# Regrouping the small matmuls of a batch in a fused attention and gated feed-forward kernel

## The chip, the cores and the metric

The kernel runs on one core of one Trainium2 chip. The metric is device microseconds of one execution. The kernel before takes 305.18 us, the median of three runs (304.89, 305.18 and 305.53 us). The profile was taken of a further execution: its trace spans 302.9 us from the first to the last instruction.

In the profile, PE is TensorE's matmul, PEld its weight load, DVE is VectorE, ACT ScalarE, POOL GpSimd, and a name with a q at its end is that engine's sequencer issuing transfers. Every fp32 matmul of the program appears as two MATMUL records, so "x4" in a timeline row is two matmuls of the program.

## The reference

Two stages. The first is a linear attention over 4 batches of 4 heads, 1088 positions and 32 dimensions; its feature map is the product of two sketches of 8 rows. The second is a feed-forward block with a sigmoid gate over all 4352 tokens.

```python
def phi(x):                                   # S1, S2: 8 x 32
    a = np.einsum('rd,bhsd->bhsr', S1, x)
    b = np.einsum('rd,bhsd->bhsr', S2, x)
    return np.einsum('bhsi,bhsj->bhsij', a, b).reshape(*x.shape[:-1], r * r)
q_p, k_p = (phi(q), phi(k))
kv = np.einsum('bhsf,bhsd->bhfd', k_p, v)
z = np.sum(k_p, axis=2)
num = np.einsum('bhsf,bhfd->bhsd', q_p, kv)
den = np.einsum('bhsf,bhf->bhs', q_p, z)[..., None] + 1e-06
attn_out = num / den
# (B,H,S,D) -> x: 4352 tokens x 128
gate = 1.0 / (1.0 + np.exp(-(x @ w_gate)))    # 128 x 1536
val = x @ w_val
out = gate * val @ w_out                      # 1536 x 128
```

All data are fp32 for the computation. The weights come as 8-byte numbers and are narrowed to fp32 on the chip, in steps that VectorE, ScalarE and GpSimd share.

## The kernel before

The feed-forward block is cut into chunks of 512 tokens. A chunk has twelve **waves**: `w1` makes one block of 128 gate columns and 128 value columns (two matmuls of 128x512, into the two banks of a PSUM tile `wave`), ScalarE takes the sigmoid, VectorE multiplies (`g`), and `w2` adds the block's share of the output (one matmul of 128x512 into `moeout`), two waves later. A **slot** runs an optional group of attention work and then so many waves; the attention of the next batch is thus woven into the waves of the batch before it.

```python
    psm = ...tile_pool(name="psm", bufs=2, space=PSUM)   # tag "wave", [P, 2, 512]: two tiles
    pso = ...tile_pool(name="pso", bufs=1, space=PSUM)   # tags "acc0", "acc1": one bank each
    ps2 = ...tile_pool(name="ps2", bufs=1, space=PSUM)   # tag "two", [P, 2, 512]: one tile

    def slot(group, waves):
        if group is not None:
            group()
        todo = moe["todo"]
        for _ in range(waves):
            more = moe["ci"] < len(tok_chk)
            if more and sum(tok_chk[moe["ci"]]) > moe["ready"]:
                break
            glu()                       # VectorE: g = value * sigmoid(gate) of the last wave
            last = moe["ci"] == len(tok_chk) - 1 and moe["w"] > 1
            lag = 3 if last else 2
            while len(todo) >= lag:
                w2(*todo.pop(0))
            if more:
                w1()
            # ... (the end of the queue)
```

`w2` also turns a finished chunk out of PSUM with a VectorE transpose (`o_sb`) and writes it out.

For each batch after the first, the denominators of all positions are made in two small matmul groups with a VectorE product between them, and the numerators in two halves of 512 and 576 positions (`n` is 0 or 1). The last step divides and writes `xT`, the feed-forward input.

```python
    def den_j(b):
        glu()
        t = ps2.tile([P, 2, 512], F32, tag="two", name="denj")
        # ... 4 matmuls of 64x160 from ZW[b] and B8[b]
        PD[b] = sbA.tile([P, 2, WD], F32, tag="pd", name="pd", bufs=1)
        nc.vector.tensor_tensor(out=PD[b], in0=t[:, :, :WD], in1=A8[b], op=MUL)

    def den_i(b):
        dps = pso.tile([P, TCH], F32, tag=f"acc{(moe['sum'] + 1) % 2}", name="deni")
        # ... 4 matmuls of 32x160 from PD[b]
        return dps

    def turn_den(b, dps):               # transpose dTi, two additions of 1e-6, one reciprocal
        # ...

    def dn(b, n, mid=None):
        t0, tn = q_chk[n]
        # ... batch 0: matmuls of the denominators, dps
        elif n == 0:
            dps = den_i(b)
        # ...
        t = ps2.tile([P, 2, 512], F32, tag="two", name="nps")
        # ... 8 matmuls of 32x256 (n = 0) or 32x288 (n = 1) from ND[b] and QP[b]

        def divide(*parts, between=None):
            # ... n == 0: turn_den; batch 0: turn, add 1e-6, reciprocal of rc
            # transpose rb <- reciprocals (spread over 32 columns)
            # between()
            # xT <- t * rb
        return divide

    def part(b, n, between=None):
        glu()
        dn(b, n)(between=between)
```

The queries' feature map is made from `cq`, which goes to DRAM and comes back with each row repeated 8 times (`spread`, tiles `qp` and `bq`); `qmult(b, n)` multiplies the two in one half. The order of a batch:

```python
    slot(None, 1)
    slot(lambda: part(0, 1, lambda: narrow_w(NJ - 1, 3)), 2)   # last weight block's final step
    v_t[1] = load_v(1)
    for b in range(1, B):
        more = b + 1 < B
        wn = 1 if b == 1 else 2
        turn_k(b)
        turn_q(b, 0)
        slot(None, wn)
        turn_q(b, 1)
        slot(lambda: begin(b), 1)
        # ... feature map of the keys, sums over positions, kv
        qmult(b, 0)
        weights_z(b)
        slot(lambda: ndt(b), 1)
        qmult(b, 1)
        load_kq(b + 1)
        slot(lambda: den_j(b), 1)
        slot(lambda: part(b, 0), wn)
        slot(None, 1)
        slot(lambda: part(b, 1), 4)
    slot(None, 10**3)
```

`narrow_w(NJ - 1, 3)` is the last of four steps that narrow the twelfth weight block; the twelfth wave reads that block.

Of the kernel before, what the change touches and what calls it, by code (L numbers as in the profile page):

```python
# [8 lines left out]
F32 = mybir.dt.float32  # L9
# [5 lines left out]
MUL = ALU.mult  # L15

P = 128
# [3 lines left out]
def kernel(  # L21
# [12 lines left out]
    nc = tc.nc  # L34

    B, H, S, D = q.shape
    R = S1.shape[0]
# [3 lines left out]
    NJ = DFF // P  # L41
# [19 lines left out]
    psm = ctx.enter_context(tc.tile_pool(name="psm", bufs=2, space=bass.MemoryType.PSUM))  # L61
# [113 lines left out]
    def narrow_w(j, step):  # L175
        if not 0 <= j < NJ:
            return
        n, jj = divmod(j, 2)
        if wide:
            if step == 0:  # L180
                narrowing[j] = narrow(
                    w_sb[:, :, j, :], w_in[n][:, :, jj], nc.gpsimd, "acc1" if j < NJ - 2 else None
                )
            next(narrowing[j])
# [205 lines left out]
    def glu():  # L390
        if moe["gate"] is not None:
            moe["gate"]()
            moe["gate"] = None
# [223 lines left out]
    def spread(b, ns, cq, put, get):  # L617
        p0 = 64 * ns[0]
        d = dram.tile([P, 2, W1], F32, tag="dq", name="dq")
        put.dma_start(out=d[p0:], in_=cq[p0:])  # L620
        for n in ns:
            for c in range(2):
                for i, t in enumerate((QP[b], BQ[b])):
                    d0 = d[64 * n + 32 * c + 2 * i, 0]
                    rows = [[8 * W1, R], [0, R]] if i == 0 else [[0, R], [8 * W1, R]]
                    get.dma_start(  # L626
                        out=t[64 * c : 64 * c + 64, n * H * W1 : (n + 1) * H * W1],
                        in_=bass.AP(
                            tensor=d0.tensor, offset=d0.offset, ap=rows + [[1, H * W1]]
                        ),  # L630
                    )

        if len(ns) < 2:
            return


        B8[b] = sbA.tile([P, W1], F32, tag="b8", name="b8", bufs=1)
        A8[b] = sbA.tile([P, 2, WD], F32, tag="a8", name="a8", bufs=1)
        for x in range(2):
            for m in range(2):  # L640
                p0 = 64 * x + 32 * m
                for i, t in enumerate((A8[b], B8[b])):
                    d0 = d[2 * i + m, 0]
                    if i == 0:
                        offset, run = d0.offset + (W1 - WD) * x, [[W1, 2], [1, WD]]
                    else:
                        offset, run = d0.offset + W1 * x, [[1, W1]]
                    put.dma_start(
                        out=t[p0 : p0 + 32],
                        in_=bass.AP(tensor=d0.tensor, offset=offset, ap=[[8 * W1, 32]] + run),  # L650
                    )
# [138 lines left out]


    def den_j(b):
        glu()
        t = ps2.tile([P, 2, 512], F32, tag="two", name="denj")
        for pi in range(2):
            rows = slice(64 * pi, 64 * pi + 64)
            for x in range(2):
                nc.tensor.matmul(  # L798
                    out=t[64 * x : 64 * x + 64, pi, :WD],
                    lhsT=ZW[b][rows].rearrange("p x i -> p (x i)"),  # L800
                    rhs=B8[b][rows, (W1 - WD) * x : (W1 - WD) * x + WD],
                    start=True,
                    stop=True,
# [7 lines that stand above are left out]
        for h in range(H):  # L811
            nc.tensor.matmul(
                out=dps[32 * h : 32 * h + 32, :WD],
                lhsT=mask["head"][:, h % 2, :],
                rhs=PD[b][:, h // 2, :],
                start=True,
                stop=True,
            )
        return dps
# [12 lines left out]
        nc.vector.reciprocal(out=RC[b], in_=RC[b])  # L832


    def dn(b, n, mid=None):
        t0, tn = q_chk[n]
        w = 32 * tn
        if b == 0:
            bank = (moe["sum"] + 1) % 2 if moe["sum"] >= 0 else 1
            dps = pso.tile([P, TCH], F32, tag=f"acc{bank}", name="dps")  # L840
        elif n == 0:
            dps = den_i(b)
        for h in range(H if b == 0 else 0):
            nc.tensor.matmul(
                out=dps[32 * h : 32 * h + 32, :w],
                lhsT=zb[:, h, :],
                rhs=half(QP[b], n)[:, 2 * (h % 2) + h // 2, :],
                start=True,
                stop=True,
            )  # L850
        if b == 0:
            dT = sbA.tile([P, 9, 32], F32, tag="dT", name="dT")
            rc = sbA.tile([P, 9, 2], F32, tag="rc", name="rc")

        def turn():
            nc.vector.transpose(out=dT[:, :tn].rearrange("p t c -> p (t c)"), in_=dps[:, :w])

        if mid is not None:
            mid(turn, rc, dT)
        t = ps2.tile([P, 2, 512], F32, tag="two", name="nps")  # L860
        for h in range(H):
            for c in range(2):
                rows = slice(64 * c, 64 * c + 64)
                nc.tensor.matmul(  # L864
                    out=t[32 * h : 32 * h + 32, c, :w],
                    lhsT=ND[b][rows, 32 * h : 32 * h + 32],
                    rhs=half(QP[b], n)[rows, 2 * (h % 2) + h // 2, :],
                    start=True,
                    stop=True,
                )  # L870

        def divide(*parts, between=None):
            if b > 0:
                if n == 0:
                    turn_den(b, dps)
                rd = RC[b][:, n]
            else:
                rd = rc
                if mid is None:
                    turn()  # L880
                    nc.vector.tensor_scalar_add(rc[:, :tn], dT[:, :tn, :2], 1e-6)
                nc.vector.reciprocal(out=rc[:, :tn], in_=rc[:, :tn])
            rb = sbA.tile([P, 9, 2, 32], F32, tag="rb", name="rb")
            for u0, u1 in parts or [(0, tn)]:
                r0 = rd[:, u0:u1]
                nc.vector.transpose(
                    out=rb[:, u0:u1].rearrange("p t c s -> p (t c s)"),
                    in_=bass.AP(
                        tensor=r0.tensor,
                        offset=r0.offset,  # L890
                        ap=[list(r0.ap[0]), [1, 2 * (u1 - u0)], [0, 32]],
                    ),
                )
                if between is not None and u0 == 0:
                    between()
                o = b * S + 64 * (t0 + u0)
                nc.vector.tensor_tensor(  # L897
                    out=xT[:, o : o + 64 * (u1 - u0)].rearrange("p (t c s) -> p c t s", c=2, s=32),
                    in0=t[:, :, 32 * u0 : 32 * u1].rearrange("p c (t s) -> p c t s", s=32),
                    in1=rb[:, u0:u1].rearrange("p t c s -> p c t s"),  # L900
                    op=MUL,
                )
            moe["ready"] = b * S + 64 * (t0 + tn)

        return divide

# [108 lines left out]
    def q01():  # L1015
        spread(0, (1,), qcomp(0, (1,), (ps2, "two")), nc.scalar, nc.sync)

    def part(b, n, between=None):
        glu()
        dn(b, n)(between=between)  # L1020

    def kv_all(b):
        kv(b, ZS[b])
# [6 lines left out]
    qmult(0, 1)  # L1030
    load_kq(1)
    slot(None, 1)
    slot(lambda: part(0, 1, lambda: narrow_w(NJ - 1, 3)), 2)
    v_t[1] = load_v(1)
    for b in range(1, B):
        more = b + 1 < B
        wn = 1 if b == 1 else 2
        turn_k(b)
        turn_q(b, 0)
        slot(None, wn)  # L1040
        turn_q(b, 1)
        slot(lambda: begin(b), 1)
        for pi in range(2):
            outer(b, pi)
            slot(None, wn)
        for step in range(2):
            sum_z(b, step)
            slot(None, wn)
            if b == 1 and step == 0:
                masks()  # L1050
        slot(lambda: kv_all(b), wn)
        if more:
            v_t[b + 1] = load_v(b + 1)
        qmult(b, 0)
        weights_z(b)
        slot(lambda: ndt(b), 1)
        qmult(b, 1)
        load_kq(b + 1)
        slot(lambda: den_j(b), 1)
        slot(lambda: part(b, 0), wn)  # L1060
        slot(None, 1)
        slot(lambda: part(b, 1), 4)
    slot(None, 10**3)


# [28 lines left out]
```

## Time and profile before

| what | value |
|---|---|
| median of three runs | 305.18 us |
| span of the profiled execution | 302.9 us |
| VectorE busy | 154.6 us (51%) |
| ScalarE busy | 80.7 us (27%) |
| GpSimd busy | 36.4 us (12%) |
| TensorE clock granted, mean | 0.998 |
| 128x512 MATMUL records, wave and moeout | 436 and 216 |

A row of a timeline has the start in us, the duration in us, the engine, the line, the operation with its tiles and shape, the number of records merged in it, and, if the engine was idle before, for how long and what ended the wait. The duration of a matmul record is modelled and reaches past the start of the next one, because matmuls are pipelined; so lengths of work on TensorE are read here from start to start, not from durations.

The span has three parts. In the first 20 us the first inputs arrive, the first weights are narrowed and batch 0 is begun. From there to about 282 us waves follow one another, with the groups of the attention between them. The last chunk, of 256 tokens, ends it.

### The profile page before, as it was taken

The page shows a single profiled execution, that of the slowest core. Times are in us where ns is not written, and L with a number is a line of the kernel's source. Part 1 is how long each engine was busy: PE and PEld are TensorE (multiplying, and loading weights), DVE is VectorE, ACT ScalarE, POOL GpSimd, SP SyncE. Part 2 cuts the span into 40 slices and gives each one's busy share as a digit, 9 for nine tenths or more (in the row PEclk, how much of TensorE's full clock was granted, in tenths as well). Part 3 has the DMA queues.
Part 4 walks back from the last instruction along what each step waited for, and adds up shares of the span by engine and source line. Part 5 has one row for each costly group of instructions (what it writes and reads, how often), then busy time and mean ns, then how long its engine had stood idle before and what let it go on. Part 6 is the DMA issues. An engine that isn't in the chain of part 4 may idle for free.

```text
span 302.9 us, 3657 instructions
## 1 busy us (share of the span) xinstructions
PE 296.3 (98%) x1363; PEld 136.3 (45%) x1363; DVE 154.6 (51%) x268; ACT 80.7 (27%) x150; POOL 36.4 (12%) x68
## 2 busy tenths in 40 slices
PE   8899999999999999999999999999999999999995
PEld 3444433443444444434444444444444444444683
DVE  6997788774645554364465541744232223222331
ACT  2556532222122222221222222221222222222220
POOL 1465550610000410000002300000000000000000
PEclk9999999999999999999999999999999999999999
DMA  7993440898201494360013990200010000100011
GB/s 216 347 339 80 126 144 6 163 204 190 98 9 25 107 196 92 61 202 0 0 20 72 182 156 2 36 2 0 0 26 8 0 0 10 27 0 0 8 30 17
DMA packets 31411, 24.24 MB, mean 80 GB/s; under 512 B 21345, under 2 KB 26593, under 8 KB 31393
## 3 DMA queue, kind: packets, MB, share of 16 engines
q1 hardware_dynamic: 27024, 16.15, 20.6%
q0 software_dynamic: 3456, 7.09, 12.4%
q10 hardware_dynamic: 912, 0.77, 0.9%
q8 instruction: 11, 0.18, 0.3%
q14 instruction: 8, 0.06, 0.1%
HBM read 20.73 MB, written 3.26 MB: 79 GB/s over the span
## 4 chain that ended last, share of the span: by engine, by line
PE 84%; DMA 9%; DVE 3%; POOL 2%; issue 1%; SPq 1%; ACT 0%; POOLq 0%; ACTq 0%
PE wave L357 52%; PE moeout L314 27%; DMA v<-in_v_dram 3%; DMA w_in<-in_moe_w_out_dram 2%; DMA bq<-dq 2%; POOL head L118 2%; DMA w_in<-in_moe_w_gate_dram 1%; PE kvz L677 1%; PE nps L864 1%; DVE w_sb L127 1%; DVE head L109 1%; PE kps L456 1%; DVE head L105 0%; PE cqps L602 0%; PE denj L798 0%
## 5 line engine op out<-in xcount | busy, mean ns | idle before, releaser
L357 PE MATMUL wave<-xT,w_sb 128*128 128x512 f32 (+1 forms) x436 | 191.7, 565 | 0.1
L381 DVE TENSOR_TENSOR g<-wave,sg 128x512 f32<-128x512 f32 x102 | 70.3, 689 | 133.3 <-ACT sg L365 133.1
L357 PEld LDWEIGHTS wave<-xT,w_sb 128*128 128x128 f32 x436 | 82.6, 190 | 93.6 <-issue 86.3
L365 ACT ACTIVATE sg<-wave 128x512 f32<-128x512 f32 x102 | 60.9, 597 | 198.9 <-PE wave L357 198.9
L314 PE MATMUL moeout<-g,w_sb 128*128 128x512 f32 (+1 forms) x216 | 105.8, 577 | 0.3 <-DVE w_sb L127 0.3
L314 PEld LDWEIGHTS moeout<-g,w_sb 128*128 128x128 f32 x216 | 39.3, 190 | 44.0 <-issue 37.1
L626 POOL DMA_DIRECT2D qp<-dq x12 | 7.1, 591 | 108.4 <-DMA dq<-cq 68.4
L118 POOL TENSOR_TENSOR head<-head,tail 128x384 int32<-128x384 int32 (+2 forms) x14 | 13.4, 955 | 18.2 <-DVE head L109 14.0
L535 DVE TENSOR_TENSOR kp<-kab 128x1152 f32<-128x1152 f32 (+2 forms) x10 | 10.5, 1068 | 0.0
L655 DVE TENSOR_TENSOR qp<-qp,bq 128x1152 f32<-128x1152 f32 (+1 forms) x7 | 9.0, 1290 | 1.3 <-DMA bq<-dq 1.3
L109 DVE SCALAR_TENSOR_TENSOR head<-cap,head 128x384 int32<-128x384 int32 (+2 forms) x14 | 7.5, 535 | 0.5
L127 DVE SCALAR_TENSOR_TENSOR w_sb<-square,head 128x384 f32<-128x384 f32 (+1 forms) x11 | 5.7, 518 | 3.9 <-POOL head L118 3.9
L258 PE MATMUL warm<-const-float32-1.0 128*128 128x512 f32 (+1 forms) x12 | 6.9, 703 | 0.8 <-PEq L1078 0.8
L626 POOL DMA_DIRECT2D bq<-dq x12 | 6.9, 576 | 0.4 <-DVE g L381 0.2
L101 ACT ACTIVATE tail<-w_in 128x384 int32<-128x384 uint32 (+1 forms) x13 | 6.6, 522 | 0.9 <-DMA w_in<-in_moe_w_gate_dram 0.7
L324 DVE STREAM_TRANSPOSE o_sb<-moeout 128x512 f32<-128x512 f32 (+1 forms) x9 | 6.1, 679 | 1.4 <-PE moeout L314 1.3
L97 POOL TENSOR_SCALAR cap<-w_in 128x384 f32<-128x384 f32 (+1 forms) x13 | 6.5, 509 | 0.0
L897 DVE TENSOR_TENSOR xT<-nps,rb 128x576 f32<-128x576 f32 (+2 forms) x9 | 5.9, 660 | 0.7
L864 PE MATMUL nps<-qp,nd 64*32 64x256 f32 (+1 forms) x128 | 5.5, 401 | 0.4 <-ACT nd L741 0.4
L436 DVE STREAM_TRANSPOSE qT<-kq 128x512 f32<-128x512 f32 (+1 forms) x8 | 5.8, 719 | 0.0
L117 ACT ACTIVATE square<-cap 128x384 f32<-128x384 f32 (+1 forms) x11 | 5.1, 463 | 1.6 <-DVE w_sb L127 1.5
L425 DVE STREAM_TRANSPOSE kT<-kq 128x1088 f32<-128x1088 f32 (+2 forms) x5 | 5.3, 1070 | 0.0
(89 smaller groups left out, 85.3 us busy)
## 6 DMA issues: line engine op xcount, KB each, us to landing
qp<-dq POOLq DMA_DIRECT2D x12, 288.0 KB, 9.6
bq<-dq POOLq DMA_DIRECT2D x12, 288.0 KB, 10.3
v<-in_v_dram SPq DMA_DIRECT2D x16, 144.0 KB, 6.5
kq<-in_k_dram SPq DMA_DIRECT2D x3, 544.0 KB, 3.8
kq<-in_q_dram SPq DMA_DIRECT2D x3, 544.0 KB, 4.7
w_in<-in_moe_w_out_dram SPq DMA_DIRECT2D x6, 256.0 KB, 7.1
w_in<-in_moe_w_gate_dram SPq DMA_DIRECT2D x5, 256.0 KB, 5.8
w_in<-in_moe_w_val_dram SPq DMA_DIRECT2D x5, 256.0 KB, 4.7
```

Source lines behind the costliest of these rows:

```text
L109: nc.vector.scalar_tensor_tensor(out=head, in0=cap, scalar=-0x40000000, in1=head, op0=ALU.bitwise_and, op1=ALU.bitwise_or)
L118: nc.gpsimd.tensor_tensor(out=head, in0=head, in1=tail, op=ALU.add)
L127: nc.vector.scalar_tensor_tensor(out=out, in0=square, scalar=1.265625 * 2.0**-30, in1=head, op0=ALU.is_ge, op1=MUL)
L258: nc.tensor.matmul(out=t[:, 0, :n], lhsT=x, rhs=r, start=True, stop=True)
L314: nc.tensor.matmul(out=moe["acc"][:, :tw], lhsT=w_sb[:, 2, j, :], rhs=g[:, jj, :tw], start=(j == 0), stop=(j == NJ - 1),)
L357: nc.tensor.matmul(out=wv[:, which, jj * tw + o : jj * tw + o + tp], lhsT=w_sb[:, which, j0 + jj, :], rhs=xT[:, t0 + o : t0 + o + tp], sta ...
L365: nc.scalar.activation(out=sg, in_=wv[:, 0], func=ACTF.Sigmoid)
L381: nc.vector.tensor_tensor(out=g, in0=wv[:, 1], in1=sg, op=MUL)
L535: eng.tensor_tensor(out=KP[b][:, pi, j0:j1].rearrange("p j m (i l) -> p (j m) i l", i=R), in0=bass.AP(tensor=a0.tensor, offset=a0.offset, ...
L626: get.dma_start(out=t[64 * c : 64 * c + 64, n * H * W1 : (n + 1) * H * W1], in_=bass.AP(tensor=d0.tensor, offset=d0.offset, ap=rows + [[1, ...
L655: nc.vector.tensor_tensor(out=q0, in0=q0, in1=half(BQ[b], n), op=MUL)
L864: nc.tensor.matmul(out=t[32 * h : 32 * h + 32, c, :w], lhsT=ND[b][rows, 32 * h : 32 * h + 32], rhs=half(QP[b], n)[rows, 2 * (h % 2) + h // ...
```

## The change

The change does four things.

1. For each batch after the first, the small matmul groups are put together. Before, `denj` stood alone, then came a wave, then `deni` with the first numerators, then one or two waves and another, then the second numerators. Now one group holds `denj`, the second numerators, `deni` and the first numerators, in this order; the second numerators stand between `denj` and `deni`, and use a `wave` tile in PSUM so that both halves can be held at once.
2. In batch 1 this group comes one slot later than `denj` did. Also one VectorE transpose of the queries (`turn_q(1, 0)`) is put behind a slot.
3. In the spread of the queries, the rows of `qp` for both halves of the partitions come in one transfer of 128 partitions instead of two of 64. `bq` stays as it was.
4. At the end of batch 0, the final narrowing step of the twelfth weight block stands ahead of the reciprocal on VectorE, rather than behind the transpose that follows it. The division's last product is put behind the next `glu`.

The purpose is to have fewer changes between wide and small matmuls, and to have the twelfth weight block ready sooner. The diff, cut to its core:

```diff
@@ spread @@
-            for c in range(2):
-                for i, t in enumerate((QP[b], BQ[b])):
+            for i, t in enumerate((QP[b], BQ[b])):
+                for c in (0, 1) if i else (0,):
                     d0 = d[64 * n + 32 * c + 2 * i, 0]
-                    rows = [[8 * W1, R], [0, R]] if i == 0 else [[0, R], [8 * W1, R]]
+                    rows = [[0, R], [8 * W1, R]] if i else [[8 * W1, 2 * R], [0, R]]
                     get.dma_start(
-                        out=t[64 * c : 64 * c + 64, n * H * W1 : (n + 1) * H * W1],
+                        out=t[64 * c : 64 * c + 64 if i else P, n * H * W1 : (n + 1) * H * W1],
@@ den_j @@
-        glu()
         t = ps2.tile([P, 2, 512], F32, tag="two", name="denj")
@@ dn @@
-    def dn(b, n, mid=None):
+    def dn(b, n, mid=None, pool=(ps2, "two")):
-        elif n == 0:
-            dps = den_i(b)
-        t = ps2.tile([P, 2, 512], F32, tag="two", name="nps")
+        t = pool[0].tile([P, 2, 512], F32, tag=pool[1], name="nps")
@@ divide @@
-        def divide(*parts, between=None):
+        def divide(*parts, first=None, between=None, later=False):
-                if n == 0:
-                    turn_den(b, dps)
+                if first is not None:
+                    first()
                 nc.vector.reciprocal(out=rc[:, :tn], in_=rc[:, :tn])
 ...
+                if later and u1 == tn:
+                    return lambda: product(u0, u1)
+                product(u0, u1)
@@ order @@
-    def part(b, n, between=None):
+    def part01(first):
         glu()
-        dn(b, n)(between=between)
+        late.append(dn(0, 1)(first=first, later=True))
+    def last01():
+        glu()
+        late.pop()()
+    def parts(b):
+        den_j(b)
+        glu()
+        divide1 = dn(b, 1, pool=(psm, "wave"))
+        dps = den_i(b)
+        divide0 = dn(b, 0)
+        turn_den(b, dps)
+        divide1()
+        divide0()
 ...
-    slot(lambda: part(0, 1, lambda: narrow_w(NJ - 1, 3)), 2)
+    slot(lambda: part01(lambda: narrow_w(NJ - 1, 3)), 1)
+    slot(last01, 1)
 ...
-        turn_q(b, 0)
+        if b > 1:
+            turn_q(b, 0)
         slot(None, wn)
+        if b == 1:
+            turn_q(b, 0)
 ...
-        slot(lambda: den_j(b), 1)
-        slot(lambda: part(b, 0), wn)
-        slot(None, 1)
-        slot(lambda: part(b, 1), 4)
+        if b == 1:
+            slot(None, 1)
+        slot(lambda: parts(b), wn + 5)
```

More of the change, by code (lines that the diff above doesn't have):

```diff
@@ L881, in divide, with product @@
                     nc.vector.tensor_scalar_add(rc[:, :tn], dT[:, :tn, :2], 1e-6)
+                if first is not None:
+                    first()
                 nc.vector.reciprocal(out=rc[:, :tn], in_=rc[:, :tn])
             rb = sbA.tile([P, 9, 2, 32], F32, tag="rb", name="rb")
+            def product(u0, u1):
+                o = b * S + 64 * (t0 + u0)
+                nc.vector.tensor_tensor(
+                    out=xT[:, o : o + 64 * (u1 - u0)].rearrange("p (t c s) -> p c t s", c=2, s=32),
+                    in0=t[:, :, 32 * u0 : 32 * u1].rearrange("p c (t s) -> p c t s", s=32),
+                    in1=rb[:, u0:u1].rearrange("p t c s -> p c t s"),
+                    op=MUL,
+                )
+                moe["ready"] = max(moe["ready"], b * S + 64 * (t0 + u1))
             for u0, u1 in parts or [(0, tn)]:
@@ L895, in divide @@
                     between()
[L896 to L903, printed above, removed]
+                if later and u1 == tn:
+                    return lambda: product(u0, u1)
+                product(u0, u1)
         return divide
@@ L1016, in q01 @@
         spread(0, (1,), qcomp(0, (1,), (ps2, "two")), nc.scalar, nc.sync)
-    def part(b, n, between=None):
+    late = []
+    def part01(first):
         glu()
-        dn(b, n)(between=between)
+        late.append(dn(0, 1)(first=first, later=True))
[11 more added lines that the diff above has]
+        divide0()
     def kv_all(b):
```

## The prediction

> **What bounds the kernel now.** I read the page's busy table first, then the chain that ended last, then TensorE's timeline around one batch, and last all engines around the two places where the change moves VectorE work.
>
> ```profile
> PE 296.3 (98%) x1363; PEld 136.3 (45%) x1363; DVE 154.6 (51%) x268; ACT 80.7 (27%) x150; POOL 36.4 (12%) x68
> ...
> PE 84%; DMA 9%; DVE 3%; POOL 2%; issue 1%; SPq 1%; ACT 0%; POOLq 0%; ACTq 0%
> ```
>
> TensorE is busy for 98% of the span and makes up 84% of the chain; the rest of the chain is almost all in the first 45 us. So from there on a change counts only if it alters the time from one matmul to the next. Nothing that VectorE, GpSimd or a transfer saves is worth anything unless TensorE was waiting for it. TensorE's timeline in batch 1 (start, duration, line, records):
>
> ```profile
> 59.55 1.02 PE L314 MATMUL moeout<-g,w_sb 128*128 128x512 f32 x2
> ...
> 62.12 1.02 PE L314 MATMUL moeout<-g,w_sb 128*128 128x512 f32 x2
> ...
> 69.96 1.88 PE L357 MATMUL wave<-xT,w_sb 128*128 128x512 f32 x4
> 71.77 0.50 PE L798 MATMUL denj<-b,zw 64*64 64x160 f32 x8
> 72.20 1.13 PE L314 MATMUL moeout<-g,w_sb 128*128 128x512 f32 x2
> 73.17 1.88 PE L357 MATMUL wave<-xT,w_sb 128*128 128x512 f32 x4
> 74.98 0.48 PE L812 MATMUL deni<-pd,head 128*32 128x160 f32 x8
> 75.39 0.66 PE L864 MATMUL nps<-qp,nd 64*32 64x256 f32 x16
> 75.98 1.12 PE L314 MATMUL moeout<-g,w_sb 128*128 128x512 f32 x2
> 76.94 1.88 PE L357 MATMUL wave<-xT,w_sb 128*128 128x512 f32 x4
> ...
> 79.52 1.88 PE L357 MATMUL wave<-xT,w_sb 128*128 128x512 f32 x4
> 81.33 0.71 PE L864 MATMUL nps<-qp,nd 64*32 64x288 f32 x16
> 81.97 1.12 PE L314 MATMUL moeout<-g,w_sb 128*128 128x512 f32 x2
> 82.94 1.88 PE L357 MATMUL wave<-xT,w_sb 128*128 128x512 f32 x4
> ```
>
> An undisturbed wave takes 62.12 - 59.55 = 2.57 us start to start: 0.86 for moeout, 1.715 for wave. Where a small group follows, wave takes longer: 71.77 - 69.96 = 1.81, so going in costs 0.095. Where a wide matmul follows a small group, moeout takes 73.17 - 72.20 = 0.97 instead of 0.86, so coming out costs 0.11. No engine is waited for at these places; the price is of the change itself, about 0.205 us for each group however small.
>
> The second place is the end of batch 0 (all engines):
>
> ```profile
> 43.46 1.00 POOL L118 TENSOR_TENSOR head<-head,tail 128x384 int32<-128x384 int32 x1 [1.63 <-DVE head L109]
> ...
> 44.52 0.27 DVE L882 RECIPROCAL rc<-rc 128x18 f32<-128x18 f32 x1
> 44.82 0.78 DVE L886 STREAM_TRANSPOSE rb<-rc 128x576 f32<-128x576 f32 x1
> 44.97 1.02 PE L314 MATMUL moeout<-g,w_sb 128*128 128x512 f32 x2
> ...
> 45.52 0.52 DVE L127 SCALAR_TENSOR_TENSOR w_sb<-cap,head 128x384 f32<-128x384 f32 x1
> ...
> 46.10 1.98 PE L357 MATMUL wave<-xT,w_sb 128*128 128x512 f32 x4
> ```
>
> This wave is the twelfth, which reads the block that w_sb writes. It was due at 44.97 + 0.86 = 45.83, but starts at 46.10, 0.06 after w_sb ends at 46.04. The reader is to see that the modelled end of moeout (45.99) hides most of this wait. Its cost is 0.27 and 0.10 more in the wave that restarts (the next moeout is at 47.92, 1.82 after it instead of 1.715).
>
> **What the Trainium skill says.** "TensorEngine Tiling (Array Packing)", Key Properties: changing the tiling mode drains TensorE. The trace agrees in kind: denj is 64*64, nps 64*32, deni 128*32, the wide ones 128*128, and each way in and out costs the 0.095 and 0.11 above. "TensorE: Matmul & The Clock Gate", Step-by-step: TensorE loads weights ahead of running matmuls only where row groups don't conflict or the background buffer is free. The 190 ns loads lie beside matmuls here (45% busy under 98%), and can't all lie beside a group of 8 short ones. "Perfetto Trace Analysis", Tensor Engine Instruction: ends of matmuls are estimates; the 0.27 us above shows it, so I count starts. "DMA: Bandwidth & Descriptors", Issuing engines are not separate DMA queues: fewer issues save only the sequencer's time. Before, an issue of qp takes GpSimd 0.59 us on the page and nothing on TensorE waits behind it.
>
> **The change part by part.**
>
> *Grouping, before.* For batch 1, against waves with nothing between: denj costs 72.20 - 71.675 + 0.11 = 0.635 (the wave was due to end at 69.96 + 1.715). deni with nps costs 75.98 - 74.885 + 0.105 = 1.20. The second nps costs 81.97 - 81.235 + 0.11 = 0.845. Sum 2.68 us. Batches 2 and 3 show the same within 0.02.
>
> *Grouping, after.* The matmuls are the same in number and shape; what goes is two ways in and two out, 2 x 0.205 = 0.41. Against it stands a new wait: deni needs pd, VectorE's product of denj, which had a whole wave to be made in and now has only the second nps. Worked out from denj's start: its modelled end is at 0.50; ScalarE started 0.06 after such an end elsewhere (kvz ends 123.72, kvd starts 123.78); pd takes 0.48; another 0.06 back to TensorE, as for w_sb. So deni can start at 1.10. The second nps, from 0.43 to 0.43 + 0.64 = 1.07, fills all of it but 0.03. The group is then 0.095 + 1.10 + 0.41 (deni) + 0.59 (nps of 256) + 0.105 = 2.30, and a batch gains 2.68 - 2.30 = 0.38.
>
> *What VectorE must have ready.* The second nps reads what qmult(b, 1) writes. In batch 1 qmult waits for a transfer and ran from 71.81 to 73.17, after denj's start; in the new order denj comes one slot of 2.57 later, at about 74, so nothing waits. This is what the extra slot is for. In batch 2 qmult ran from 130.34 to 131.69, and denj starts at 131.68, nps 0.43 later: no wait. In batch 3:
>
> ```profile
> 190.25 0.71 DVE L324 STREAM_TRANSPOSE o_sb<-moeout 128x512 f32<-128x512 f32 x1
> ...
> 193.23 1.35 DVE L655 TENSOR_TENSOR qp<-qp,bq 128x1152 f32<-128x1152 f32 x1
> ```
>
> Here a chunk ended just before, and its transpose took VectorE's time. Batch 2 now spends 7 waves after denj, not 8, so in batch 3 the chunk's end falls a wave later, into the slot right ahead of the group. The queue is then: g after the sigmoid (ends at 192.19) to 192.85, o_sb to 193.5, qmult to 194.8. The second nps could start at 194.17 + 0.43 = 194.60, but starts at 194.86; pd, behind qmult, ends near 195.25, and deni starts near 195.5 rather than 195.27. That takes back 0.2, and leaves 0.18 in batch 3.
>
> *Buffers.* The second nps takes a wave tile. The wave two further on needs that tile, and so the second division's product. From deni's end VectorE has dTi 0.34, two additions 0.25, reciprocal 0.38, transpose 0.78 and product 0.76 with gaps of 0.04, near 2.8 us; TensorE comes back to the tile after nps, a wave and moeout, 0.6 + 2.68 + 0.86 = 4.1 us. No wait. deni's bank is wanted by moeout only where a chunk begins there, in batch 3; dTi is through about when nps ends, so at most 0.1.
>
> *Narrowing step.* w_sb at 44.52 instead of 45.52 ends at 45.04, long before 45.83: gain 0.37. The delayed product ends near 47.6; the wave that reads it is due at 48.4.
>
> *Transfers and the moved transpose.* 12 qp issues become 6. TensorE waits for none of them in the traces of batches 2 and 3. Counted as 0.
>
> Sum: 0.37 + 0.38 + 0.38 + 0.18 = 1.31 us. 305.18 - 1.31 = 303.87, say 303.9.
>
> **The rivals.** *The pd wait grows.* If the semaphore from TensorE to VectorE and back costs 0.3 more than I read, in each batch, all but 0.4 us of the gain is lost: 304.7. For it: pd never followed denj directly, so its start after denj isn't seen (in batch 2 it began at 133.03, behind g). Against it: the 0.06 at kvd. *The small groups get cheaper side by side.* If most of a switch's cost belongs to the wide weight load (190 ns), then denj and the second nps, now followed by narrow ones, shorten too, by up to 0.1 each; pd's wait would swallow most of it. That makes 303.6. *qmult becomes the bound in every batch.* If the transfers of bq land later than before, since qp's larger transfer stands ahead of them, batch 1's group waits: VectorE already idles 1.3 us for bq there. The new slot leaves about 1.2 us of room; beyond it TensorE would stall one for one, and 1 us lost gives 304.9. *Nothing is gained*, because TensorE's other waits take over: the list of what TensorE waited for has no row after 46 us (its largest, 0.8 us, is at the start), so I give this little.
>
> **Range and chances.** The terms that I trust are the 0.37 and the six ways in and out (1.23); the uncertain ones are waits of 0 to 0.3 a batch, and the medians' own spread of 0.3. I take 303.2 to 304.8. Two per cent is 6.1 us, four times all that the change touches on the chain; so faster 0.01, same 0.98, slower 0.01. That it is faster at all I hold at 0.88.
>
> **What would show it.** In the profile after: the twelfth wave 0.86 after its moeout (right) or a later start behind another VectorE row (wrong). In each batch one row sequence denj, nps, deni, nps with one start of moeout at 0.97 after it. deni 1.05 to 1.15 after denj in batches 1 and 2, and about 0.2 more in batch 3 with qmult just ahead. From the wave ahead of denj to the wave after nps, 2.30 above undisturbed waves in batches 1 and 2. It would be wrong if deni stood more than 0.3 later than said, if the second nps waited for qp in batch 1, or if a wave after the group waited for a division.

## The result, and the profile after

The changed kernel takes 303.49 us (median of four runs, 303.37 to 304.15), the kernel before beside it 305.03 (304.70 to 305.53). The ratio is 0.9952, with a 95% interval from 0.9932 to 0.9973: a gain of 0.8 to 2.1 us. A second comparison, on the chip of the last four experiments, gave 303.75 (nine runs) against 304.82 (33 runs), ratio 0.9965, from 0.9952 to 0.9979.

The page of the changed kernel, its busy table and its chain by engine:

```profile
PE 295.3 (98%) x1363; PEld 137.3 (46%) x1363; DVE 154.7 (51%) x268; ACT 80.7 (27%) x150; POOL 33.0 (11%) x62
...
PE 86%; DVE 5%; DMA 3%; issue 2%; POOL 2%; ACT 1%; SPq 0%; DVEq 0%; POOLq 0%; ACTq 0%
```

TensorE has as many records as before and is 1.0 us shorter busy. The modelled durations of neighbouring records overlap, so what went is not work but time from one start to the next. Its timeline around the group, in batch 1 and then only the group in batches 2 and 3:

```profile
72.11 1.88 PE L357 MATMUL wave<-xT,w_sb 128*128 128x512 f32 x4
73.92 0.50 PE L797 MATMUL denj<-b,zw 64*64 64x160 f32 x8
74.36 0.72 PE L861 MATMUL nps<-qp,nd 64*32 64x288 f32 x16
75.13 0.48 PE L811 MATMUL deni<-pd,head 128*32 128x160 f32 x8
75.54 0.66 PE L861 MATMUL nps<-qp,nd 64*32 64x256 f32 x16
76.13 1.13 PE L314 MATMUL moeout<-g,w_sb 128*128 128x512 f32 x2
77.09 1.88 PE L357 MATMUL wave<-xT,w_sb 128*128 128x512 f32 x4
...
130.99 0.50 PE L797 MATMUL denj<-b,zw 64*64 64x160 f32 x8
131.42 0.72 PE L861 MATMUL nps<-qp,nd 64*32 64x288 f32 x16
132.11 0.48 PE L811 MATMUL deni<-pd,head 128*32 128x160 f32 x8
132.52 0.66 PE L861 MATMUL nps<-qp,nd 64*32 64x256 f32 x16
...
190.54 0.50 PE L797 MATMUL denj<-b,zw 64*64 64x160 f32 x8
191.20 0.72 PE L861 MATMUL nps<-qp,nd 64*32 64x288 f32 x16 [0.15 <-DVE qp L655]
191.85 0.48 PE L811 MATMUL deni<-pd,head 128*32 128x160 f32 x8
192.26 0.66 PE L861 MATMUL nps<-qp,nd 64*32 64x256 f32 x16
```

There is one way in (72.11 to 73.92, 1.81) and one way out (76.13 to 77.09, 0.96). deni starts after denj by 1.21 us in batch 1, 1.12 in batch 2 and 1.31 in batch 3. All engines at the end of batch 0, and VectorE in batches 1 and 3:

```profile
44.44 0.56 DVE L127 SCALAR_TENSOR_TENSOR w_sb<-cap,head 128x384 f32<-128x384 f32 x1
44.91 0.26 DVE L881 RECIPROCAL rc<-rc 128x18 f32<-128x18 f32 x1
44.92 1.02 PE L314 MATMUL moeout<-g,w_sb 128*128 128x512 f32 x2
...
45.78 1.88 PE L357 MATMUL wave<-xT,w_sb 128*128 128x512 f32 x4
45.91 0.65 DVE L381 TENSOR_TENSOR g<-wave,sg 128x512 f32<-128x512 f32 x1
46.49 0.74 DVE L886 TENSOR_TENSOR xT<-nps,rb 128x576 f32<-128x576 f32 x1
...
70.01 1.35 DVE L655 TENSOR_TENSOR qp<-qp,bq 128x1152 f32<-128x1152 f32 x1
...
74.49 0.49 DVE L805 TENSOR_TENSOR pd<-denj,a 128x320 f32<-128x320 f32 x1 [1.72 <-DMA kq<-in_k_dram]
...
74.90 0.68 DVE L381 TENSOR_TENSOR g<-wave,sg 128x512 f32<-128x512 f32 x1
...
189.20 0.70 DVE L324 STREAM_TRANSPOSE o_sb<-moeout 128x512 f32<-128x512 f32 x1
189.83 1.32 DVE L655 TENSOR_TENSOR qp<-qp,bq 128x1152 f32<-128x1152 f32 x1
...
191.12 0.49 DVE L805 TENSOR_TENSOR pd<-denj,a 128x320 f32<-128x320 f32 x1
```

The twelfth wave starts 0.86 after its moeout. In batch 1 the product of the queries starts at 70.01 without a wait. In batch 3 it stands behind o_sb, ends at 191.15, and the second numerators start 0.05 after that.

One more step of the change belongs here, since deni waits for pd: `glu` now stands behind `den_j`, so on VectorE pd comes ahead of g (74.49 and 74.90). Before, g came first (in batch 2 at 132.42, pd at 133.03). No run tests this order by itself.

**How the runs are compared below.** A whole run contains a start-up whose length differs by chance: the first moeout started anywhere from 19.04 to 19.93 us in the fourteen profiles here, all of the same program up to there. So each run is judged by the time from the first moeout to the start of the last row of moeout, called its *length*. It covers everything that the change touches. The kernel before: 296.39 - 19.26 = 277.13. The changed kernel: 295.18 - 19.23 = 275.95; the same kernel a second time: 295.11 - 19.18 = 275.93. So the length repeats within 0.02 in these two, and the change is worth 1.18 us of it.

| run | length, us | against |
|---|---|---|
| before | 277.13 | |
| changed kernel | 275.95 | before: -1.18 |
| narrowing step alone | 276.83 | before: -0.30 |
| joined transfer alone | 277.09 | before: -0.04 |
| no slot in batch 1 | 275.94 | changed: -0.01 |
| no slot, two transfers | 275.96 | changed: +0.01 |
| slot, two transfers | 276.85 | changed: +0.90 |
| the same again | 275.94 | changed: -0.01 |
| group split | 277.06 | changed: +1.11 |
| deni straight behind denj | 277.22 | changed: +1.27 |
| queries' product early | 275.76 | changed: -0.19 |
| mask on VectorE | 275.86 | changed: -0.09 |
| both of these | 275.68 | changed: -0.27 |

### The profile page after: what moved, and what is told of

Same layout as the page of the kernel before. It is cut to its first block, busy times and chain, and to the rows that moved or that the text cites. A ratio compares the mean times of both kernels' runs of the same rounds, so it can differ in the third digit from the quotient of the medians.

```text
span 301.7 us, 3642 instructions
## 1 busy us (share of the span) xinstructions
PE 295.3 (98%) x1363; PEld 137.3 (46%) x1363; DVE 154.7 (51%) x268; ACT 80.7 (27%) x150; POOL 33.0 (11%) x62
## 3 DMA queue, kind: packets, MB, share of 16 engines
q0 software_dynamic: 2592, 7.08, 10.5%
## 4 chain that ended last, share of the span: by engine, by line
PE 86%; DVE 5%; DMA 3%; issue 2%; POOL 2%; ACT 1%; SPq 0%; DVEq 0%; POOLq 0%; ACTq 0%
PE wave L357 52%; PE moeout L314 27%; DMA bq<-dq 2%; PE nps L861 2%; POOL head L118 1%; PE kvz L677 1%; DVE head L109 1%; DVE w_sb L127 1%; DVE qp L655 1%; DMA s_in<-in_S_dram 1%; PE kps L456 1%; DVE head L105 1%; PE cqps L602 0%; PE deni L811 0%; PE dps L841 0%
## 5 line engine op out<-in xcount | busy, mean ns | idle before, releaser
L627 POOL DMA_DIRECT2D qp<-dq x6 | 3.5, 583 | 105.9 <-DMA dq<-cq 105.9
L535 DVE TENSOR_TENSOR kp<-kab 128x1152 f32<-128x1152 f32 (+2 forms) x10 | 10.5, 1070 | 0.0
```

The costliest lines, as they stand in the source:

```text
L535: eng.tensor_tensor(out=KP[b][:, pi, j0:j1].rearrange("p j m (i l) -> p (j m) i l", i=R), in0=bass.AP(tensor=a0.tensor, offset=a0.offset, ...
L627: get.dma_start(out=t[64 * c : 64 * c + 64 if i else P, n * H * W1 : (n + 1) * H * W1], in_=bass.AP(tensor=d0.tensor, offset=d0.offset, ap ...
```

## The experiments

### The narrowing step alone

On the kernel before; `first` is the narrowing step, and the division's last product stays ahead of g:

```diff
-        def divide(*parts, between=None):
+        def divide(*parts, between=None, first=None):
 ...
+                if first is not None:
+                    first()
                 nc.vector.reciprocal(out=rc[:, :tn], in_=rc[:, :tn])
 ...
-    def part(b, n, between=None):
+    def part(b, n, first=None):
         glu()
-        dn(b, n)(between=between)
+        dn(b, n)(first=first)
```

> The kernel before with one thing changed: the last narrowing step of the twelfth weight block ahead of the reciprocal. Theory: the twelfth wave starts 0.86 us after its moeout instead of 1.13, and the wave after it takes no extra 0.10; so from the start of the eleventh wave's moeout on everything on TensorE is 0.37 us earlier than in the kernel before, and the rest is as before. Rival: VectorE's delay is only moved, since the reciprocal and the transpose now run later and hold back the division that the first wave of the second chunk needs; then that wave starts late and the gain is below 0.1 us.

The length is 0.30 shorter. Of this, 0.03 lies ahead of the edited place: `dps`, a matmul group of batch 0, starts 21.73 us after the first moeout, in the kernel before 21.76. From the twelfth wave's moeout to kps of batch 1 it took 5.35 us instead of 5.62, a gain of 0.27: the twelfth wave was on time, but one 0.10 stayed. The timeline of this run:

```profile
45.53 0.19 PEld L357 LDWEIGHTS wave<-xT,w_sb 128*128 128x128 f32 x1 [0.24 <-DVE rc L884]
45.96 1.88 PE L357 MATMUL wave<-xT,w_sb 128*128 128x512 f32 x4
...
46.27 0.76 DVE L899 TENSOR_TENSOR xT<-nps,rb 128x576 f32<-128x576 f32 x1
46.95 0.68 DVE L381 TENSOR_TENSOR g<-wave,sg 128x512 f32<-128x512 f32 x1
...
47.68 0.30 PEld L314 LDWEIGHTS moeout<-g,w_sb 128*128 128x128 f32 x2 [0.67 <-DVE g L381]
47.68 1.12 PE L314 MATMUL moeout<-g,w_sb 128*128 128x512 f32 x2
48.64 1.88 PE L357 MATMUL wave<-xT,w_sb 128*128 128x512 f32 x4
```

moeout started when it was due (45.96 + 1.715), yet took 0.96 to the wave instead of 0.86. Its operand g, behind the division on VectorE, ended at 47.63, only 0.05 before. The weight load shows what is different: that of the wave at 45.96 starts 0.43 ahead of its matmul, that of this moeout waits for g and starts with it. In the changed kernel the division's last product is put behind g, g ends at 46.56, the load starts at 47.06 for a moeout at 47.49, and the 0.10 is gone: from moeout to kps it takes 5.24. The rival was right that VectorE's delay is moved, and wrong on what it hits and how hard; the deferred product, which the prediction valued at nothing, is worth this 0.10. It has no run of its own.

The same sign stands at every way out of a small group: the wide load starts with the moeout behind the group (in the changed kernel both at 76.13), where an undisturbed one starts 0.43 ahead, and in the kernel before at the wave that restarts late (load at 46.09, wave at 46.10). All of these lose about 0.10. A load that starts only 0.22 ahead loses nothing (36.27, wave at 36.49, next moeout 1.72 after it, in the kernel before). That the late load is what costs it fits all three places, but no run separates it from the change of shape.

### The transfers and the slot: four runs and a repeat

The joined transfer alone, on the kernel before:

```diff
-            for c in range(2):
-                for i, t in enumerate((QP[b], BQ[b])):
+            for i, t in enumerate((QP[b], BQ[b])):
+                for c in (0, 1) if i else (0,):
 ...
-                    rows = [[8 * W1, R], [0, R]] if i == 0 else [[0, R], [8 * W1, R]]
+                    rows = [[0, R], [8 * W1, R]] if i else [[8 * W1, 2 * R], [0, R]]
 ...
-                        out=t[64 * c : 64 * c + 64, n * H * W1 : (n + 1) * H * W1],
+                        out=t[64 * c : 64 * c + 64 if i else P, n * H * W1 : (n + 1) * H * W1],
```

> The kernel before with one thing changed: qp's rows in one transfer of 128 partitions. Theory: VectorE's wait for bq in batch 1 is gone, as in all runs with the joined transfer so far, but TensorE never waited for it in this order of groups; so from the first moeout to the last row of moeout TensorE takes the 277.13 us of the kernel before within 0.05. Rival: the joined transfer is worth something on TensorE by itself, 0.2 us or more.

Length 277.09, within 0.05 of before. The product in the kernel before, and then in this run:

```profile
71.81 1.36 DVE L655 TENSOR_TENSOR qp<-qp,bq 128x1152 f32<-128x1152 f32 x1 [1.30 <-DMA bq<-dq]
...
70.95 1.35 DVE L655 TENSOR_TENSOR qp<-qp,bq 128x1152 f32<-128x1152 f32 x1
```

VectorE's wait for bq was gone, and nothing was gained on TensorE.

The changed kernel without the slot:

```diff
-        if b == 1:
-            slot(None, 1)
-        slot(lambda: parts(b), wn + 5)
+        slot(lambda: parts(b), wn + 5 + (b == 1))
```

> The changed kernel without the extra slot in batch 1: the group of small matmuls stands a wave earlier, at about 71.35 us, and the waves after it are one more. Theory 1 (the joined transfer of qp brings bq earlier, the product of the queries in batch 1 ran from 70.01 to 71.36 us in the changed kernel and not from 71.8): the second numerators, due at 71.35 + 0.43 = 71.78 us, wait for nothing, and the end on TensorE is within 0.1 us of the changed kernel. Theory 2 (as the prediction had it: the slot is what spares the wait): the numerators wait about 1 us and the end is about 1 us later.

Length 275.94: denj at 71.53, the numerators at 71.97 as if nothing were to be waited for, since the product of the queries had ended at 71.54. Theory 1 holds, and with the joined transfer the slot does nothing in this run.

The same without the joined transfer (the diff above turned round as well):

> The changed kernel without the extra slot in batch 1 and with qp's rows in two transfers of 64 partitions as before. Theory 1 (the joined transfer brings bq earlier): the product of the queries in batch 1 waits for bq until about 71.4 us (71.8 in the kernel before, less the 0.43 gained by then) and ends at about 72.7; the second numerators, due at 71.8, start at about 72.8, so the end is 0.9 to 1.0 us later than with the joined transfer and no slot. Theory 2 (landing times of bq do not depend on how qp is cut): no difference from the run without the slot and with the joined transfer.

The product waited for bq, but only by 0.38, until 70.74; the numerators started 0.10 late and pd's wait behind them swallowed it (deni again 1.21 after denj). The length is the same, 0.02 apart, as theory 2 had it. The product did wait, as theory 1 had it, but too briefly to cost anything.

With the slot and without the joined transfer:

> The changed kernel with its extra slot in batch 1, but qp's rows in two transfers of 64 partitions as before. Theory 1: VectorE waits for bq in batch 1 by 1.0 to 1.5 us again, and TensorE does not, because the slot leaves 2.57 us; the end is within 0.1 us of the changed kernel. Theory 2 (the transfers are worth something on TensorE even with the slot): the end is 0.3 us or more later.

Here the wait was long:

```profile
69.74 0.69 DVE L381 TENSOR_TENSOR g<-wave,sg 128x512 f32<-128x512 f32 x1 [1.19 <-ACT sg L365]
...
73.70 1.36 DVE L654 TENSOR_TENSOR qp<-qp,bq 128x1152 f32<-128x1152 f32 x1 [3.27 <-DMA bq<-dq]
74.27 0.50 PE L796 MATMUL denj<-b,zw 64*64 64x160 f32 x8
...
74.98 0.68 DVE L381 TENSOR_TENSOR g<-wave,sg 128x512 f32<-128x512 f32 x1
...
75.72 0.72 PE L860 MATMUL nps<-qp,nd 64*32 64x288 f32 x16 [0.95 <-DVE g L381]
```

VectorE stood 3.27 us for bq, and g of a finished wave stood behind it in VectorE's order. The numerators want that wave's PSUM tile, so they start 0.06 after g's end (75.66), not after the product's (75.06). denj to nps is 1.45 us instead of 0.44. The end is 0.90 later, which is theory 2's outcome. Theory 1 had the wait at 1.0 to 1.5 us; it was longer than the slot could cover. Repeated and timed:

> The changed kernel with qp's rows in two transfers of 64 partitions, again and timed. In the single look it took 276.85 us from the first moeout to the last row of moeout, 0.90 more than the changed kernel, since VectorE waited 3.27 us for bq in batch 1; the run without the slot waited only 0.38. Theory 1 (with the two transfers the landing of bq in batch 1 differs from run to run by some us, by chance): the times of the rounds spread over 0.5 us or more, and their median is 0.2 to 1.0 us above the changed kernel's. Theory 2 (the long wait was a single event): the median is within 0.15 us of the changed kernel's.

The profile of the repeat has a wait of 1.97 us for bq and a length of 275.94, so the slot covered it: the product ended at 73.40 and the numerators started at 74.33. Without the slot they would have been due 2.57 earlier, so by these numbers an estimate of their wait there is 1.7 us. The median of 22 runs is 303.61, 0.14 below the changed kernel's, but four of the 22 lie at 304.56, 304.69, 304.94 and 307.36, while none of the changed kernel's 13 is above 304.16. So theory 2 is right on the median and theory 1 on the spread. The run with the wait of 3.27 took 304.78, like three of these four; but none of the four was profiled, so it isn't shown that bq made them late, and the slowest also had a lower mean clock (0.987).

In all, five profiles with two transfers show waits for bq of 1.30, 0.55, 0.38, 3.27 and 1.97 us, and nine profiles with the joined one show none. Counted from the first moeout, VectorE got bq at 51.2 to 54.1 us with two transfers, and with the joined one it was there at 50.8 us in eight of the nine profiles (in the ninth VectorE came for it only at 51.1). So the joined transfer lands bq earlier in these profiles and spares VectorE a wait of changing length, which made the length longer in one of the five. No profile with the joined transfer had bq late enough to need the slot.

### The group split

```diff
     def parts(b):
 ...
-        divide1 = dn(b, 1, pool=(psm, "wave"))
+        divide0 = dn(b, 0, pool=(psm, "wave"))
         dps = den_i(b)
-        divide0 = dn(b, 0)
         turn_den(b, dps)
-        divide1()
         divide0()
+
+    def parts1(b):
+        glu()
+        dn(b, 1)()
 ...
-        slot(lambda: parts(b), wn + 5)
+        slot(lambda: parts(b), 2)
+        slot(lambda: parts1(b), wn + 3)
```

> The changed kernel, but in each batch the group is cut in two: denj, the first numerators and deni stay together, the second numerators come two waves later as a group of their own. Theory 1 (each group costs a way in and a way out, 0.205 us, and nothing else was saved): three more groups cost 3 x 0.205 = 0.62 us; the first numerators are 0.05 us shorter than the second, so deni waits 0.05 more in batches 1 and 2, about 0.7 us later in all than the changed kernel. Theory 2 (what grouping saved is VectorE's order, not the switches of TensorE): the end is within 0.2 us of the changed kernel.

1.11 us, more than the 0.7 expected. Counted as what each batch adds to plain waves (from the wave ahead of a group to the wave behind it, less 2.575 us for an undisturbed one), batches 1 and 2 took 2.66 and 2.57 instead of 2.41 and 2.32: 0.25 each, as expected. Batch 3 took 3.11 instead of 2.51, for a reason that I had left out:

```profile
192.53 0.35 DVE L823 STREAM_TRANSPOSE dTi<-deni 128x160 f32<-128x160 f32 x1
...
192.94 1.13 PE L314 MATMUL moeout<-g,w_sb 128*128 128x512 f32 x2 [0.47 <-DVE dTi L823]
```

A chunk begins right there, in the bank that deni has just used, and must wait until dTi has read it. It was due 0.41 after deni's start at 191.99, so it starts 0.54 late. In the changed kernel the first numerators stand between deni and this moeout and hide the wait. Batch 3 also got 0.19 back: the first numerators don't read the late product, and deni comes 1.12 after denj instead of 1.31. The switch price of 0.205 a group is borne out by batches 1 and 2.

### deni straight behind denj

```diff
-        divide1 = dn(b, 1, pool=(psm, "wave"))
         dps = den_i(b)
+        divide1 = dn(b, 1, pool=(psm, "wave"))
         divide0 = dn(b, 0)
```

> The changed kernel with deni straight behind denj in each group, and both numerators after it: the wait for VectorE's product pd lies bare. Theory 1 (deni cannot start before 1.10 us after denj, whatever stands between): TensorE idles about 0.65 us between denj and deni in batches 1 and 2, and both numerators come after that; 0.6 us later per batch in batches 1 and 2 and 0.5 in batch 3, where the product of the queries held the numerators anyway; 1.7 us in all. Theory 2 (the wait for pd is shorter than read, and it is the length of the numerators that set deni's start): 0.3 us per batch or less, under 1 us in all.

Batch 2 of this run:

```profile
131.42 0.50 PE L797 MATMUL denj<-b,zw 64*64 64x160 f32 x8
...
131.99 0.49 DVE L805 TENSOR_TENSOR pd<-denj,a 128x320 f32<-128x320 f32 x1 [0.56 <-PE denj L797]
...
132.54 0.48 PE L811 MATMUL deni<-pd,head 128*32 128x160 f32 x8 [0.61 <-DVE pd L805]
132.95 1.15 PE L861 MATMUL nps<-qp,nd 64*32 64x288 f32 x32
...
134.03 1.13 PE L314 MATMUL moeout<-g,w_sb 128*128 128x512 f32 x2
```

deni starts 1.12 after denj, with nothing between: exactly as with the numerators between. So theory 1 holds, the pd wait and not the numerators sets deni's start in batch 2. The total is 1.27 and not 1.7, because the two numerators side by side take 1.08 us (132.95 to 134.03), where apart they take 0.65 + 0.59 = 1.24 (in the split run and in the changed kernel, both ahead of a wide matmul). They have the same shape of tile, 64*32, so the shape changes once less, and that saves 0.16. The kernel before has such a pair too, kps and cqps of batch 2, both 64*32 with 288 columns: kps, followed by its like, takes 0.51 us, and cqps, followed by a wide matmul, 0.62 (starts at 97.62, 98.13 and 98.75). What the change from nps to deni alone costs isn't shown, for there deni waits for pd.

Not tried: deni last, behind both numerators, where no shape would change between these. The numerators in the tile `two` would then wait until pd has been read from denj's tile, so a further tile would be needed to gain by it.

### The queries' product early, the mask on VectorE, and both

```diff
+        if b > 1:
+            qmult(b, 1)
         slot(lambda: kv_all(b), wn)
 ...
-        qmult(b, 1)
+        if b == 1:
+            qmult(b, 1)
         load_kq(b + 1)
```

> The changed kernel with the product of the queries' second half moved ahead of the key-value slot in batches 2 and 3, where VectorE idles. Theory 1 (in batch 3 the second numerators wait for this product, which stands behind a finished chunk's transpose): in batch 3 the numerators start 0.43 us after denj instead of 0.66 and deni 1.12 after it instead of 1.31; the end is 0.19 us earlier. Theory 2 (the transpose, not the product, delays pd, and pd sets deni's start): deni stays at about 1.3 us after denj and nothing is gained.

Exactly as theory 1 has it, 0.19 us. Batch 3 of this run:

```profile
189.58 0.70 DVE L324 STREAM_TRANSPOSE o_sb<-moeout 128x512 f32<-128x512 f32 x1
190.92 0.50 PE L797 MATMUL denj<-b,zw 64*64 64x160 f32 x8
...
191.36 0.71 PE L861 MATMUL nps<-qp,nd 64*32 64x288 f32 x16
191.50 0.49 DVE L805 TENSOR_TENSOR pd<-denj,a 128x320 f32<-128x320 f32 x1 [1.21 <-PE denj L797]
...
192.04 0.48 PE L811 MATMUL deni<-pd,head 128*32 128x160 f32 x8
```

o_sb is where it was, but VectorE is free long before denj ends; nps follows denj by 0.44 and deni by 1.12.

```diff
-        nc.gpsimd.memset(mask["head"], 0.0)
+        nc.vector.memset(mask["head"], 0.0)
 ...
-            nc.gpsimd.tensor_copy(
+            nc.vector.tensor_copy(
                 out=mask["head"][:, m, :8].rearrange("p (k g) -> p k g", k=2),
```

> The changed kernel with the head mask of deni made on VectorE rather than GpSimd. In batch 1 deni starts 1.21 us after denj although pd ends at 1.06; in batch 2 it starts 1.12 after denj, 0.06 after pd's end. Theory 1 (in batch 1 deni is the first to read the mask and so waits for two engines' semaphores, which costs 0.09 us by itself though the mask is long there): deni in batch 1 starts 1.12 us after denj and the end is 0.09 us earlier. Theory 2 (first-time cost of another kind): deni stays at 1.21.

Length 0.09 shorter. Batch 1 of this run, TensorE alone:

```profile
74.62 0.50 PE L797 MATMUL denj<-b,zw 64*64 64x160 f32 x8
75.06 0.72 PE L861 MATMUL nps<-qp,nd 64*32 64x288 f32 x16
75.74 0.48 PE L811 MATMUL deni<-pd,head 128*32 128x160 f32 x8
```

deni comes 1.12 after denj, as in batch 2. The mask had been in place for over 10 us in the changed kernel too; what went is the second engine to wait for. deni is still the first to read the mask, so theory 2 falls.

> The changed kernel with both mends that were seen to work singly: the product of the queries' second half ahead of the key-value slot in batches 2 and 3 (0.19 us), and the head mask made on VectorE (0.09 us). Theory: the two are in different batches and add up; from the first moeout to the last row of moeout TensorE takes 275.67 us, 0.28 less than the changed kernel's 275.95, and deni starts 1.12 us after denj in all three batches. In the medians of whole runs this is at the edge of what can be seen. Rival: one takes back the other's gain, for the mask's work on VectorE delays another step of batch 1: then under 0.15 us.

Length 275.68, 0.27 below the changed kernel, and deni 1.12 after denj in all three batches: the two add up. The medians are 303.62 (nine runs) against 303.75 of the changed kernel beside it, which by themselves couldn't be told apart; its ratio to the kernel before is 0.9958, from 0.9944 to 0.9972.

> The changed kernel itself, beside the others on the same chip. From the first moeout to the last row of moeout TensorE takes 275.95 us within 0.05, and VectorE doesn't wait for bq in batch 1. Against the kernel before the median is 1.2 to 1.5 us lower.

Length 275.93, and no wait for bq. Its median is 1.07 below the kernel before, a little under what I wrote.

## Why the prediction was right, and where not

The time (303.9) and the range hold; the worked-out gain of 1.31 us stands against 1.18 in length and 1.54 and 1.07 in the two comparisons of medians. The two medians' gains differ by 0.47, more than any single term below, so the terms are judged by the traces.

- *TensorE's gaps are all that counts*: right. Every gain and loss above is one between two matmul rows; taking VectorE's wait for bq away by itself left the length at 277.09.
- *Narrowing step, 0.37*: the size is right in the changed kernel, 0.38 (from the twelfth wave's moeout to kps of batch 1 it takes 5.24 us, before 5.62). But the step credited only the earlier w_sb, which alone gives 0.27; the rest is the deferred product, which the sum had at 0. So the number is right and its cause half named.
- *Grouping, batch 2, 0.38*: right, 0.36. The group adds 2.32 to the waves; the prediction said 2.30.
- *Batch 1, 0.38*: mis-sized, 0.27. The term "deni can start at 1.10" measured 1.21 there. The sum knew one wait, pd's; deni in batch 1 also waits for GpSimd, which made the mask, and that costs 0.09 though GpSimd was long done. With the mask on VectorE it is 1.12.
- *Batch 3, 0.18 after a stall of 0.2*: right, 0.17, and for the reason given; moving the product away gives the 0.19 back.
- *Extra slot in batch 1*: the prediction's reading, that the slot is what spares the wait, fell for the kernel as changed. With the joined transfer the product is done (71.54) before the numerators want it (71.97) even without the slot. With two transfers the slot did cover a wait of 1.97 us, and not one of 3.27. The part "Transfers, counted as 0" was right for the length and the median, but left out that bq's landing moves from run to run: the rival that the joined transfer would make bq later came out the other way round.
- *Rival, small groups cheaper side by side*: shapes that are alike are cheaper (1.08 for 1.24), but in the group as built no two alike are neighbours, and denj in front of nps takes 0.43 as it did in front of a wide matmul. "TensorEngine Tiling (Array Packing)", Key Properties, of the Trainium skill ties the drain to a change of tiling mode and doesn't speak of wide or small; that the saving of 0.16 came where two groups of one shape stood side by side agrees with it.
- *Rival, the pd wait grows*: no; 1.12 for 1.10.
- *Buffers*: right for the wave tile. deni's bank was put at up to 0.1 and costs nothing in the changed kernel, but 0.54 once the first numerators no longer hide it.

## What to carry to other kernels

When one engine is busy from end to end, count its starts and not its durations: each way into and out of a group of another tile shape cost TensorE about 0.1 us here that no wait shows, so groups are best put together, and like shapes next to like. Whatever then stands between two dependent groups should be as long as the round trip through the other engine, here 1.12 us from denj to deni. And once groups are packed, look at what stands ahead in VectorE's order, since a late transfer there also holds back unrelated results (g, in the run with the wait of 3.27 us) and with them the PSUM tiles that the packed groups need.

## What was not expected of the hardware

- A matmul started on time and still lost 0.10 us when its operand had arrived only 0.05 us before (moeout at 47.68 with g at 47.63). Its weight load then started with it rather than 0.43 ahead.
- A wait for a second engine that had finished over 10 us earlier cost 0.09 us on TensorE (deni in batch 1 at 1.21 after denj, 1.12 with the mask on VectorE).
- The same bytes in one transfer of 128 partitions instead of two of 64 took 2592 packets instead of 3456 on GpSimd's queue, and 10.5% of the engines' time instead of 12.4%, and the last piece of bq then came without any wait in nine profiles, against waits of 0.38 to 3.27 us in five. Whether it is the packets or the earlier issue (the last bq transfer of batch 1 issued at 57.7 us, not 59.2) wasn't told apart.
